# Holding prefetches behind urgent reads in a fused Fourier-mixing and ReGLU kernel

## The chip, the cores and the metric

The kernel runs on one core of a Trainium2 chip. The metric is the device time of one execution in microseconds (us), lower is better. Engines are named as in the profile: PE is TensorE (PEld its weight loads), DVE VectorE, ACT ScalarE, POOL GpSimd, SP SyncE; SPq and POOLq are the instruction streams of SP and POOL that issue DMAs.

## The reference, cut to what matters

```python
# x: 8 batches x 3008 positions x 256 channels, float32
X = np.fft.rfft(x, axis=1)
Y = X * (filt_r + 1j * filt_i)            # one filter per frequency and channel
x = np.fft.irfft(Y, n=3008, axis=1).reshape(8 * 3008, 256)
gate = np.maximum(x @ w_gate, 0.0)        # 256 -> 1536
out = (gate * (x @ w_val)) @ w_out        # 1536 -> 256
```

The kernel does the transform as two short ones, 3008 = 94 x 32. Per batch there are three stages, with a trip through device memory between them since the axes change places:

- Stage A: a product over the 94 (psA), written to `Abuf`.
- Stage B: `Abuf` is read back as the tile `at`; a product over the 32 (psX), the multiplication with the filters `Ftr` and `Fti` (tt, uu), and the product back (psD), written to `Dbuf`.
- Stage C: `Dbuf` is read back as `dC`; the product back over the 94 (psY) gives yT, the input of the gated layer.

The gated layer (psV, psG, psO) is the bulk of TensorE's work. It runs in a main loop of 47 blocks of 12 steps; the stages of the next batch are strewn between these steps. Only batch 0's stages, and part of batch 1's stage A, stand ahead of the loop, in a prologue.

## The kernel before

These are the parts that the change and the argument touch; cuts are marked with `# ...`.

```python
def load_x(b, engs, cut=None):             # x of one batch: XF[0], XF[1], 1.57 MB each, 3 DMAs each
    # ...
def load_filters():
    for src, dst in FILT:                  # (filt_r, Ftr), (filt_i, Fti)
        for a in range(2):
            # ... two DMAs: the main parts
        nc.gpsimd.dma_start(dst[64:95:2, NG - 2:, :], ...)     # two small ones
        # ...
        nc.gpsimd.dma_start(nyq[-1], ...)

def hold_gpsimd(tile_):                    # GpSimd issues nothing more until tile_ is there
    scr = pro.tile(list(tile_.shape), tile_.dtype, tag="scr", bufs=3)
    nc.gpsimd.tensor_copy(scr, tile_)

def load_at(b, c):                         # one quarter of stage B's input
    if c == 0:
        ats[b] = sb.tile([128, NG, D], BF16, tag="at", bufs=1, name="at")
    nc.sync.dma_start(ats[b][32 * c:32 * c + 32], _ap(Abuf[b], ...))

# ---- prologue
load_x(0, (nc.scalar, nc.sync), 2 * q)
# ...
hold_gpsimd(XF[0][:, 2 * q - 8:2 * q])     # first quarter of x
load_filters()
warm(14)                                   # filler products, 512 columns each
for i, f in enumerate(items_a(0)):         # stage A of batch 0
    f()
    warm(1, 256)
    # ... load_tables(), load_at(0, 0..2)
load_at(0, 3)
warm(22)
# ... place_tables, place_filter
hold_gpsimd(ats[0][96:128, NG - 1, 0:8])
load_vg(0, DFF // 3)
nc.sync.dma_start(gate, ats[0][96:128, NG - 1, 0:8])
load_x(1, (nc.sync,))
early = items_a(1)
def amid(i):                               # in stage B of batch 0
    if i < 8:
        warm(1)
    else:
        next(early)()
for f in items_b(0, amid):
    f()
load_d(0, 0, 2)
# ... a small DMA of Dbuf on gpsimd, so that what follows is held
load_vg(DFF // 3, DFF)
load_o()
for i in range(8):
    next(early)()
    warm(1, 256)
for h in range(2):
    item_c(0, h)
load_d(0, 2)

# ---- what is strewn into the main loop
C_AT = (8, 10)
for b in range(1, B):
    end = (b * S // W - 1) * NFT + C_AT[0] - 5
    s0, sb0 = (0, 13) if b == 1 else (end - 54, end - 30 | 1)
    # ... stage A from step s0
    for c in range(4):
        at_step(s0 + n - 10 + 4 * c if b > 1 else 4, lambda b=b, c=c: load_at(b, c))
    if b + 1 < B:
        at_step(sb0 + 3, lambda b=b: load_x(b + 1, (nc.gpsimd,)))
    for i, f in enumerate(items_b(b)):     # stage B from step sb0
        at_step(sb0 + 2 * i, f)
    at_step(sb0 + 27, lambda b=b: load_d(b))
```

In program order the load of the next x stands after the start of stage B. GpSimd, which issues it, does not run in that order: it has nothing else to do and issues each half of x as soon as stage A has read the buffer that it goes into.

Of the kernel before, what the change touches and what calls it, by code (L numbers as in the profile page):

```python
# [12 lines left out]
FP32 = mybir.dt.float32  # L13
# [18 lines left out]
NG = 24  # L32
# [3 lines left out]
def _ap(t, offset_elems, ap_list):  # L36
    return dataclasses.replace(
        t, offset=t.offset + offset_elems, ap=[list(p) for p in ap_list]
    )
# [63 lines left out]
def kernel(  # L103
# [10 lines left out]
    nc = tc.nc  # L114
# [16 lines left out]
    sb = ctx.enter_context(tc.tile_pool(name="sb", bufs=2))  # L131
    ps = ctx.enter_context(tc.tile_pool(name="ps", bufs=2, space=bass.MemoryType.PSUM))
    prologue = ExitStack()
    pro = prologue.enter_context(tc.tile_pool(name="pro", bufs=1))
# [6 lines left out]
    XF = [consts.tile([128, NX2 * D], FP32, name=f"XF{c}") for c in range(N2 // NX2)]  # L141
# [11 lines left out]
    def load_x(b, engs, cut=None):  # L153
        w = NX2 * D
        n = 0
        for c, xf in enumerate(XF):
            for (c0, c1) in ((0, w),) if cut is None or c else ((0, cut), (cut, w)):
                for m in range(3):
                    rows = min(32, B * N1 - (b * N1 + 32 * m))
                    n += 1  # L160
                    engs[n % len(engs)].dma_start(xf[m:m + 4 * rows - 3:4, c0:c1],  # L161
                                                  _ap(x, (b * N1 + 32 * m) * N2 * D + c * w + c0,
                                                      [[N2 * D, rows], [1, c1 - c0]]))

    H = NG // 2
    FILT = ((filt_r, Ftr), (filt_i, Fti))
# [8 lines left out]
    def place_tables(half):  # L175
        gs = slice(half * H, half * H + H)
        for a in range(2):
            nc.vector.tensor_scalar(F2[:, gs, a * 64:a * 64 + 64], tabs[:, half, 0],
                                    WA[:, NROW + a:NROW + a + 1], None, op0=ALU.mult)
            for i, t in ((1, I2t), (2, I2u)):  # L180
                nc.vector.tensor_scalar(
                    t[:, gs, :].rearrange("p g (n a c) -> p g n a c", a=2, c=2)[:, :, :, a, :],
                    tabs[:, half, i].rearrange("p g (n c) -> p g n c", c=2),
                    WA[:, NROW + 2 + a:NROW + 3 + a], None, op0=ALU.mult)
# [3 lines left out]
    def load_filters():  # L188

        for src, dst in FILT:  # L190
            for a in range(2):
                r, k1, n = a * 64, 1 + 24 * a, NG - 2 * a
                nc.gpsimd.dma_start(dst[r:r + 31:2, 0:n, :],
                                    _ap(src, k1 * D, [[N1 * D, 16], [1, n * D]]))
                nc.gpsimd.dma_start(dst[r + 1:r + 32:2, 0:n, :],
                                    _ap(src, (N1 - k1) * D, [[N1 * D, 16], [-D, n], [1, D]]))
            nc.gpsimd.dma_start(dst[64:95:2, NG - 2:, :],
                                _ap(src, 0, [[N1 * D, 16], [47 * D, 2], [1, D]]))
            nyq.append(pro.tile([1, D], BF16, tag="nyq", bufs=2, name="nyq"))
            nc.gpsimd.dma_start(nyq[-1], _ap(src, (S // 2) * D, [[D, 1], [1, D]]))  # L200
# [20 lines left out]

    def hold_gpsimd(tile_):

        scr = pro.tile(list(tile_.shape), tile_.dtype, tag="scr", bufs=3)
        nc.gpsimd.tensor_copy(scr, tile_)


    turn = {"tags": ("fft", "psv", "psg", "pso"), "i": 0}
# [1 line left out]
    def fft_tag():  # L230
        turn["i"] += 1
        return turn["tags"][turn["i"] % len(turn["tags"])]

    def items_a(b):

        def one(c, j, st):
            if j == 0:
                st["asb"] = sb.tile([NROW, NC2 * D], BF16, tag="asb", bufs=4, name="asb")
            psA = ps.tile([128, 512], FP32, tag=fft_tag(), name="psA")
            o = (c * NC2 % NX2) * D + j * 512  # L240
            nc.tensor.matmul(psA[0:NROW], WA[:, :NROW], XF[c * NC2 // NX2][:, o:o + 512],  # L241
                             start=True, stop=True)
            dst = st["asb"][:, j * 512:(j + 1) * 512]
            nc.scalar.copy(dst, psA[0:NROW])  # L244
            if j == 3:
                nc.sync.dma_start(_ap(Abuf[b], c * NROW * NC2 * D, [[NC2 * D, NROW], [1, NC2 * D]]),
                                  st["asb"])
        for c in range(N2 // NC2):
            st = {}
            for j in range(NC2 * D // 512):  # L250
                yield lambda c=c, j=j, st=st: one(c, j, st)
# [3 lines left out]
    ats = {}  # L255

    def load_at(b, c):
        if c == 0:
            ats[b] = sb.tile([128, NG, D], BF16, tag="at", bufs=1, name="at")
        nc.sync.dma_start(ats[b][32 * c:32 * c + 32],  # L260
                          _ap(Abuf[b], c * NROW * NC2 * D, [[D, 32], [4 * NC2 * D, NG], [1, D]]))

    def items_b(b, amid=None):
# [36 lines left out]
        for g in range(0, NG, 2):  # L300
            def both(g=g):
                fwd(g)
                if amid:
                    amid(g // 2)
                if len(held) > 2:
                    inv()
            yield both
# [5 lines left out]
    def load_d(b, z0=0, z1=NZ):  # L313
        for z in range(z0, z1):
            dC = sb.tile([NROW, 4, D], BF16, tag="dC", bufs=12)
            nc.sync.dma_start(dC, _ap(Dbuf[b], z * 4 * NROW * D,
                                      [[D, NROW], [NROW * D, 4], [1, D]]))
            dCs[b, z] = dC
# [68 lines left out]
    def warm(n, cols=512):  # L387

        psJ = ps.tile([128, 512], FP32, tag=fft_tag(), name="psJ")
        for i in range(n):  # L390
            nc.tensor.matmul(psJ[:, :cols], junk[:, 0:128], junk[:, :cols], start=True, stop=True)  # L391

    nc.sync.dma_start(WA, nc.inline_tensor(wa_h, name="dft_wa").ap())
    q = NX2 * D // 4
# [7 lines left out]
    load_x(0, (nc.scalar, nc.sync), 2 * q)  # L402
    for (src, dst) in FILT:
        nc.vector.memset(dst[64:128, NG - 2:, :], 0.0)
    hold_gpsimd(XF[0][:, 2 * q - 8:2 * q])
    load_filters()

    warm(14)
# [5 lines left out]
        if i % 4 == 3 and i > 3:  # L414
            load_at(0, i // 4 - 1)
    load_at(0, 3)
    warm(22)
    place_tables(0)
    place_tables(1)
    for fi in range(2):  # L420
# [2 lines left out]
    for fi in range(2):  # L423
        place_filter(fi, 0, 1, nc.scalar.copy)
        place_filter(fi, 1, 1, nc.vector.tensor_copy)
# [3 lines that stand above are left out]
# [3 lines left out]

    def amid(i):
        if i < 8:
            warm(1)
        else:
            next(early)()

    for f in items_b(0, amid):
        f()  # L440
# [17 lines left out]
    def at_step(s, f):  # L458
        side.setdefault(s, []).append(f)
# [5 lines that stand above are left out]
        a_items = early if b == 1 else items_a(b)  # L465
        n = 0
        for i, f in enumerate(a_items):
            at_step(s0 + i, f)
            n += 1
        for c in range(4):  # L470
            at_step(s0 + n - 10 + 4 * c if b > 1 else 4, lambda b=b, c=c: load_at(b, c))
        if b + 1 < B:
            at_step(sb0 + 3, lambda b=b: load_x(b + 1, (nc.gpsimd,)))
        for i, f in enumerate(items_b(b)):
            at_step(sb0 + 2 * i, f)
        at_step(sb0 + 27, lambda b=b: load_d(b))
# [42 lines left out]
```

## Time and profile before

The median is 1015.6 us (1014.9 to 1016.7). The profiled execution has a span of 1014.0 us.

| where TensorE waits for `at` | wait, us |
|---|---|
| batch 0 (prologue) | 7.67 |
| batch 1 | 15.65 |
| batches 3, 4, 5, 6 | 4.84, 2.85, 2.38, 4.78 |
| batches 2, 7 | under 1, 0 |

Two parts of the page of the kernel before matter here: busy time by engine, and the chain of work that ended last.

```profile
span 1014.0 us, 16145 instructions
PE 951.2 (94%) x5906; PEld 566.4 (56%) x6016; DVE 546.2 (54%) x823; ACT 527.0 (52%) x940; POOL 42.0 (4%) x70
...
PE 85%; DMA 11%; issue 1%; DVE 1%; ACT 1%; SPq 0%; POOL 0%; ACTq 0%
```

TensorE is the bottleneck nearly everywhere; the chain leaves it for 11% of the span, to follow DMAs. The table of waits of TensorE in the kernel before says which (total us, number of waits, longest).

```profile
PE psX L273 <- DMA at<-Abuf: 38.2, 6, 15.6
PE psA L241 <- DMA XF<-in_x_dram: 2.7, 1, 2.7
PE psJ L391 <- DVE junk L397: 2.5, 1, 2.5
PE psO L372 <- ACT osb L378: 2.5, 2, 2.0
```

Nearly all of it is stage B waiting for its input. (In batch 2 the profile names no releaser for the wait, and it is not in this table.) Here is batch 3 in the timeline of TensorE, kernel before. The columns are start, duration (merged over the instructions of the line), engine, line, operation, result and operands, count, and in brackets the idle time ahead of it and what ended it.

```profile
347.21 0.60 PE L354 MATMUL psV<-yT,WvT 128*128 128x512 bf16 x2
347.64 0.59 PE L354 MATMUL psG<-yT,WgT 128*128 128x512 bf16 x2
348.07 0.60 PE L372 MATMUL psO<-WoT,prod 128*128 128x256 bf16 x4
353.52 0.59 PE L273 MATMUL psX<-at,F 128*128 128x256 bf16 x2 [4.84 <-DMA at<-Abuf]
353.89 1.06 PE L354 MATMUL psV<-yT,WvT 128*128 128x512 bf16 x2
```

Besides the wait there is a second cost. The pair of products that took 0.60 us from first start to last end takes 1.06 us after the wait: the clock has been halved. From start to start it is 0.86 us against 0.43.

What delayed `at`? First the queue of SP around batch 3, then the issues of GpSimd, then SP's queue in batch 7, which has no next x; all of the kernel before.

```profile
337.39 1.52 SPq L246 DMA_DIRECT2D Abuf<-asb  x1
349.54 0.32 SPq L260 DMA_DIRECT2D at<-Abuf  x1
```

```profile
319.25 1.58 POOL L161 DMA_DIRECT2D XF<-in_x_dram  x3 [99.74 <-PE psA L241]
337.04 1.57 POOL L161 DMA_DIRECT2D XF<-in_x_dram  x3 [16.21 <-PE psA L241]
```

```profile
831.85 0.32 SPq L246 DMA_DIRECT2D Abuf<-asb  x1
837.60 0.32 SPq L260 DMA_DIRECT2D at<-Abuf  x1
```

SP issues the last quarter of `at` when the last quarter of `Abuf` has been written. With x issued 0.35 us ahead of it, that write (0.39 MB) takes 12.1 us; in batch 7, without x, 5.7 us. The x that is in the way will be used some 100 us later.

### The profile page before, as it was taken

Reading aid. Unit: us, or ns where it says so; the run is one execution under the profiler, and the core shown is the slowest. Engines: PE = TensorE matmul, PEld = TensorE weight load, DVE = VectorE, ACT = ScalarE, POOL = GpSimd, SP = SyncE. Lnnn points to the kernel's source line nnn. Section 1 sums busy time; section 2 is a strip of 40 time slices with the busy share of each in tenths; the row PEclk is TensorE's granted clock in tenths of the full one; section 3 lists DMA queues with packets and bytes.
Section 4 is the critical chain, followed back from the end, with each engine's and each line's share of the span. In section 5 each row is a group of like instructions: output and inputs, shape, how many; then the busy total and the mean of one; then the engine's idle time right before and its main releaser. Section 6 shows DMA issues by size and latency. Waiting matters only on the chain.

```text
span 1014.0 us, 16145 instructions
## 1 busy us (share of the span) xinstructions
PE 951.2 (94%) x5906; PEld 566.4 (56%) x6016; DVE 546.2 (54%) x823; ACT 527.0 (52%) x940; POOL 42.0 (4%) x70
## 2 busy tenths in 40 slices
PE   7693999999999899998999989999799999999995
PEld 3341666556665466645665456655466556666664
DVE  3632765347653376534865358543575437755552
ACT  3561555555555455554555545555365555555552
POOL 3330000000000000000000000001000000000000
PEclk9796999999999999999999999999899999999999
DMA  9899132261234412454222551416324232241111
GB/s 263 224 227 236 53 100 57 64 223 52 75 98 149 141 39 78 96 158 133 63 78 71 160 141 54 124 51 170 101 58 122 60 99 64 55 110 41 32 32 43
DMA packets 94432, 106.29 MB, mean 105 GB/s; under 512 B 7796, under 2 KB 84724, under 8 KB 92660
## 3 DMA queue, kind: packets, MB, share of 16 engines
q1 hardware_dynamic: 87520, 80.03, 29.8%
q0 software_dynamic: 6240, 22.71, 8.1%
q10 hardware_dynamic: 592, 2.51, 0.7%
q8 instruction: 47, 0.77, 0.3%
q14 instruction: 33, 0.27, 0.1%
HBM read 59.32 MB, written 49.81 MB: 108 GB/s over the span
## 4 chain that ended last, share of the span: by engine, by line
PE 85%; DMA 11%; issue 1%; DVE 1%; ACT 1%; SPq 0%; POOL 0%; ACTq 0%
PE psG L354 22%; PE psO L372 22%; PE psV L354 21%; PE psA L241 10%; DMA Abuf<-asb 7%; DMA at<-Abuf 3%; PE psX L273 2%; PE psD L293 2%; PE psD L292 2%; PE psY L338 2%; DMA XF<-in_x_dram 1%; DMA out_dram<-osb 1%; ACT vsb L357 0%; DVE prod L359 0%; PE psJ L391 0%
## 5 line engine op out<-in xcount | busy, mean ns | idle before, releaser
L359 DVE SCALAR_TENSOR_TENSOR prod<-psG,vsb 128x512 bf16<-128x512 f32 x564 | 390.1, 692 | 374.9 <-ACT vsb L357 357.6
L357 ACT CAST vsb<-psV 128x512 bf16<-128x512 f32 x564 | 331.3, 587 | 252.5 <-PE psV L354 209.8
L372 PE MATMUL psO<-WoT,prod 128*128 128x256 bf16 x2256 | 338.8, 274 | 4.0 <-ACT osb L378 2.5
L354 PE MATMUL psG<-yT,WgT 128*128 128x512 bf16 x1098 | 331.4, 381 | 4.4 <-DMA WgT<-in_moe_w_gate_dram 0.6
L354 PE MATMUL psV<-yT,WvT 128*128 128x512 bf16 x1049 | 321.7, 382 | 1.7 <-ACT yT L343 0.6
L372 PEld LDWEIGHTS <-prod 128*128 128x128 bf16 x2256 | 221.7, 98 | 148.7 <-issue 6.4
L354 PEld LDWEIGHTS <-WgT 128*128 128x128 bf16 x1128 | 110.6, 98 | 136.9 <-issue 4.4
L354 PEld LDWEIGHTS <-WvT 128*128 128x128 bf16 x1128 | 104.8, 98 | 60.2 <-issue 49.7
L241 PE MATMUL psA<-XF,WA 128*96 128x512 f32 x256 | 129.6, 592 | 2.7 <-DMA XF<-in_x_dram 2.7
L244 ACT CAST asb<-psA 96x512 bf16<-96x512 f32 x128 | 74.4, 582 | 104.8 <-PE psA L241 101.4
L276 DVE TENSOR_TENSOR tt<-psX,Ftr 128x512 bf16<-128x512 f32 x96 | 65.5, 683 | 38.4 <-PE psX L273 38.3
L295 ACT CAST dsb<-psD 128x512 bf16<-128x512 f32 x96 | 56.1, 587 | 52.9 <-PE psD L293 51.4
L273 PE MATMUL psX<-at,F 128*128 128x256 bf16 x192 | 38.5, 284 | 39.1 <-DMA at<-Abuf 38.2
L378 ACT COPY osb<-psO 128x512 f32<-128x512 f32 (+1 forms) x96 | 55.4, 577 | 33.7 <-PE psO L372 26.1
L282 DVE TENSOR_TENSOR uu<-psX,Fti 128x512 bf16<-128x512 f32 x90 | 61.3, 681 | 0.0
L293 PE MATMUL psD<-uu,I2u 128*128 128x256 bf16 x192 | 47.7, 275 | 0.5 <-POOL uu L280 0.5
L292 PE MATMUL psD<-tt,I2t 128*128 128x256 bf16 x192 | 47.8, 276 | 0.0
L161 POOL DMA_DIRECT2D XF<-in_x_dram x36 | 19.0, 532 | 625.6 <-PE psA L241 625.4
L273 PEld LDWEIGHTS <-F 128*128 128x128 bf16 x192 | 18.9, 100 | 43.9 <-issue 25.6
L338 PEld LDWEIGHTS <-dC 96*128 96x128 bf16 x604 | 35.3, 99 | 13.5 <-issue 10.8
L241 PEld LDWEIGHTS psA<-XF,WA 128*96 128x96 f32 x256 | 35.1, 163 | 12.2 <-issue 5.9
L345 DVE CAST yT<-psY 128x512 bf16<-128x512 f32 x47 | 32.2, 685 | 17.8 <-PE psY L338 17.8
(45 smaller groups left out, 181.8 us busy)
## 6 DMA issues: line engine op xcount, KB each, us to landing
XF<-in_x_dram POOLq DMA_DIRECT2D x34, 512.0 KB, 8.4
Abuf<-asb SPq DMA_DIRECT2D x32, 384.0 KB
at<-Abuf SPq DMA_DIRECT2D x32, 384.0 KB
dC<-Dbuf SPq DMA_DIRECT2D x64, 192.0 KB
Dbuf<-dsb SPq DMA_DIRECT2D x31, 384.0 KB
out_dram<-osb SPq DMA_DIRECT2D x72, 94.0 KB
XF<-in_x_dram SPq DMA_DIRECT2D x8, 512.0 KB
tabs<-dft_tab ACTq DMA_DIRECT2D x2, 576.0 KB
```

The lines of the kernel that those rows point to most:

```text
L241: nc.tensor.matmul(psA[0:NROW], WA[:, :NROW], XF[c * NC2 // NX2][:, o:o + 512], start=True, stop=True)
L244: nc.scalar.copy(dst, psA[0:NROW])
L273: nc.tensor.matmul(psX[:, i], F2[:, g + i, :], at[:, g + i, :], start=True, stop=True)
L276: nc.vector.tensor_tensor(tt, psX, Ftr[:, g:g + 2, :], op=ALU.mult)
L282: nc.vector.tensor_tensor(uu, psX, Fti[:, g:g + 2, :], op=ALU.mult)
L292: nc.tensor.matmul(psD[:, i], I2t[:, g + i, :], tt[:, i], start=True, stop=False)
L293: nc.tensor.matmul(psD[:, i], I2u[:, g + i, :], uu[:, i], start=False, stop=True)
L295: nc.scalar.copy(st["dsb"][:, o:o + 2, :], psD)
L354: nc.tensor.matmul(pt[:, :W], w[:, h, ft * 128:(ft + 1) * 128], yt[:, h, :], start=(h == 0), stop=(h == 1))
L357: nc.scalar.copy(vsb, psV[:, :W])
L359: nc.vector.scalar_tensor_tensor(prod, in0=psG[:, :W], scalar=0.0, in1=vsb, op0=ALU.max, op1=ALU.mult)
L372: nc.tensor.matmul(psO[:, t % 2], prods[ft][:, t * 128:(t + 1) * 128], WoT[:, ft, :], start=(ft == 0), stop=(ft == NFT - 1))
```

## The change

The intent is to let urgent transfers go first. The next x is held, by a small copy on GpSimd, until the last quarter of `at` has landed. In the prologue the filters are held until the first half of x (before: its first quarter) has landed, and their large parts are issued ahead of the small ones. Then there are two tunings of fillers, products on a constant tile that are meant to keep TensorE's clock up: 26 instead of 22 ahead of stage B of batch 0, and 128 instead of 512 columns within it. The whole diff:

```diff
--- before.py
+++ after.py
@@ -194,6 +194,7 @@
                                     _ap(src, k1 * D, [[N1 * D, 16], [1, n * D]]))
                 nc.gpsimd.dma_start(dst[r + 1:r + 32:2, 0:n, :],
                                     _ap(src, (N1 - k1) * D, [[N1 * D, 16], [-D, n], [1, D]]))
+        for src, dst in FILT:
             nc.gpsimd.dma_start(dst[64:95:2, NG - 2:, :],
                                 _ap(src, 0, [[N1 * D, 16], [47 * D, 2], [1, D]]))
             nyq.append(pro.tile([1, D], BF16, tag="nyq", bufs=2, name="nyq"))
@@ -221,8 +222,8 @@
 
     def hold_gpsimd(tile_):
 
-        scr = pro.tile(list(tile_.shape), tile_.dtype, tag="scr", bufs=3)
-        nc.gpsimd.tensor_copy(scr, tile_)
+        scr = sb.tile([128, 8], FP32, tag="scr", bufs=2)
+        nc.gpsimd.tensor_copy(scr[:tile_.shape[0]], tile_)
 
 
     turn = {"tags": ("fft", "psv", "psg", "pso"), "i": 0}
@@ -402,7 +403,7 @@
     load_x(0, (nc.scalar, nc.sync), 2 * q)
     for (src, dst) in FILT:
         nc.vector.memset(dst[64:128, NG - 2:, :], 0.0)
-    hold_gpsimd(XF[0][:, 2 * q - 8:2 * q])
+    hold_gpsimd(XF[0][:, 4 * q - 8:])
     load_filters()
 
     warm(14)
@@ -414,7 +415,7 @@
         if i % 4 == 3 and i > 3:
             load_at(0, i // 4 - 1)
     load_at(0, 3)
-    warm(22)
+    warm(26)
     place_tables(0)
     place_tables(1)
     for fi in range(2):
@@ -432,7 +433,7 @@
 
     def amid(i):
         if i < 8:
-            warm(1)
+            warm(1, 128)
         else:
             next(early)()
 
@@ -470,7 +471,10 @@
         for c in range(4):
             at_step(s0 + n - 10 + 4 * c if b > 1 else 4, lambda b=b, c=c: load_at(b, c))
         if b + 1 < B:
-            at_step(sb0 + 3, lambda b=b: load_x(b + 1, (nc.gpsimd,)))
+            def next_x(b=b):
+                hold_gpsimd(ats[b][96:128, NG - 1, 0:8])
+                load_x(b + 1, (nc.gpsimd,))
+            at_step(sb0 + 1, next_x)
         for i, f in enumerate(items_b(b)):
             at_step(sb0 + 2 * i, f)
         at_step(sb0 + 27, lambda b=b: load_d(b))
```

## The prediction

> **What bounds the kernel now.** TensorE: busy 951 of 1014 us (page, part 1), 85% of the chain that ended last. In the table of waits it waits 38.2 us, six times, in front of stage B's first product (psX) for the DMA that lands its input (at<-Abuf). By batch, from the timeline: 7.67 us (batch 0), 15.6 (1), none to speak of in 2, 4.84, 2.85, 2.38, 4.78 (3 to 6), none in 7. Batch 7 is the only one with no further x to load. Its last Abuf write took 5.7 us from its issue until the read behind it could be issued; in batches 3 to 6 the same write took 12.1, 10.3, 9.8 and 12.1 us, with the second half of the next x issued within 0.5 us of it. So x's 3 MB is in the way of 0.8 MB that is urgent.
>
> The waits also cost clock. After the 4.84 us wait two 128x512 matmuls take 0.85 us instead of 0.43 for about 4.5 us. The Trainium skill ("TensorE: Matmul & The Clock Gate", The HAM clock gate) says an idle window of about 3.4 us halves the clock until it has been busy that long; the trace agrees: 2.38 us left no mark, 2.85 us some (about 1.7 us lost).
>
> **Later batches.** The change holds x behind the landing of the last quarter of at; x is used some 100 us later. Written in 5.7 us and read in 3.9, at arrives about 1.4 us ahead of TensorE in batches 3 to 6. Waits saved: 14.9 us; cold clock: about 2.2+1.7+2.2, say 6. Together 21 us, all on TensorE's chain. The holds are 0.2 us copies on idle GpSimd. x will now run beside Dbuf and output writes; at most 1 us of that comes back.
>
> **Batch 1.** From 60 to 98 us the DMA engines are saturated (busy share about 1.0 in the windows) and move 9.3 MB, of which x is 3.1. At the 277 GB/s that GpSimd's queue reaches for its own share, x is worth 11 us. So at lands at about 87 instead of 98.3, while TensorE arrives at 82.7: some 4 us of wait stay, since weights and dC are still in front. Saved: 11 us of wait and 1 of cold clock: 12.
>
> **Start, batch 0.** Holding the filters until XF[0] is complete (about 2.5 us later) gives x the engines: the 2.7 us wait of psA for the second half of x should mostly go. But DMA is saturated from 7 to about 33 us, and filters and tables are needed before stage B too, so the wait for at mostly moves: stage B starts 2 us earlier. Fillers of 128 instead of 512 columns save 0.32 us (cold) or 0.16 (warm) each, at most 1.9 us over eight; batch 1's x, needed at 48.8, may take part of that back. warm(26) adds 0.9 us inside a wait: nothing. Together 3 us (0 to 6).
>
> **Sum.** 21 + 12 + 3 = 36, less 1 for contention: about 980 us. Range 969 to 992. Faster by over 2%: 0.94; within 2%: 0.05; slower: 0.01.
>
> **What would show it.** Waits of psX for at: about 0 in batches 3 to 6, 0 to 6 us in batch 1, 4 to 8 in batch 0. Last Abuf write of batches 3 to 6 about 6 us. GpSimd's x issues right after at has landed. psA's wait for x under 1 us.
>
> **What would make it wrong.** Output writes or Dbuf writes, not x, slow the Abuf writes; the late x stalls the output buffers; late filters hold stage B of batch 0; batch 1's weights alone keep at beyond 90 us.

## The result and the profile after

The changed kernel takes 984.8 us in the median (984.2 to 986.1, 4 runs) against 1015.6 us. The ratio is 0.9697, with a 95% interval of 0.9681 to 0.9714. (Ratios are the mean time of one kernel's fast runs over that of the other's of the same rounds, so not quite the ratio of the medians.)

The same parts of the page, and the table of waits of TensorE, for the changed kernel:

```profile
span 982.2 us, 16279 instructions
PE 951.0 (97%) x6020; PEld 565.2 (58%) x6020; DVE 544.9 (55%) x823; ACT 526.7 (54%) x940; POOL 42.9 (4%) x76
...
PE 91%; DMA 5%; SPq 1%; ACT 0%; issue 0%; DVE 0%; POOL 0%; ACTq 0%; POOLq 0%
```

```profile
PE psX L274 <- DMA at<-Abuf: 16.3, 3, 8.2
...
PE psO L373 <- ACT osb L379: 2.5, 2, 2.0
PE psD L294 <- POOL uu L281: 1.5, 2, 1.0
PE psG L355 <- DMA WgT<-in_moe_w_gate_dram: 1.3, 1, 1.3
```

TensorE's busy time looks the same to 0.2 us, but these two figures can't be compared: 110 products are missing from the records of the kernel before (5906 products for 6016 weight loads), none from these. In the second profile of the changed kernel (see below), where 110 are missing too, TensorE is busy for 944.8 us, 6.4 us less than before. So some of the gain is in the products themselves, which ran at the low clock for less time; the rest is waits. The waits for `at` fell from 38.2 to 16.3 us. psA's wait for x (2.7 us) is gone in this profile, and small new waits stand in its place, for GpSimd's product uu and for weights. The wait for output buffers (psO for osb) is as it was, so the later x did not stall them.

GpSimd's issues around batch 3, and SP's last write and read of batches 3 and 5, changed kernel:

```profile
339.09 0.18 POOL L226 CAST scr<-at 32x8 f32<-32x8 bf16 x1 [118.04 <-DMA at<-Abuf]
339.60 3.16 POOL L161 DMA_DIRECT2D XF<-in_x_dram  x6 [0.33 <-PE psX L274]
```

```profile
326.92 1.43 SPq L247 DMA_DIRECT2D Abuf<-asb  x1
334.69 0.32 SPq L261 DMA_DIRECT2D at<-Abuf  x1
...
564.12 0.32 SPq L247 DMA_DIRECT2D Abuf<-asb  x1
569.85 0.32 SPq L261 DMA_DIRECT2D at<-Abuf  x1
```

x now leaves 0.5 us after `at` has landed. The last write takes 7.8, 6.1, 5.7 and 5.6 us in batches 3 to 6, as against 12.1, 10.3, 9.8 and 12.1. Batch 3 keeps a wait of 0.79 us, batches 4 to 6 none.

Where the 31.8 us of the two profiles came from is read best from the start of stage B of each batch, in the timelines of TensorE of both kernels:

| first psX of batch | before, us | changed, us | lead, us |
|---|---|---|---|
| 0 | 38.76 | 37.36 | 1.4 |
| 1 | 98.34 | 89.55 | 8.8 |
| 2 | 230.39 | 219.92 | 10.5 |
| 3 | 353.52 | 339.00 | 14.5 |
| 4 | 477.17 | 457.13 | 20.0 |
| 5 | 599.51 | 575.27 | 24.2 |
| 6 | 722.58 | 693.40 | 29.2 |
| 7 | 843.00 | 811.53 | 31.5 |
| end | 1014.0 | 982.2 | 31.8 |

Batches 3 to 7 give 21.0 us (31.5 less 10.5), batch 1 with the low clock after it and the wait of 0.95 us in batch 2, which went too, 9.1 (10.5 less 1.4), and the start 1.4 us. What is left in the changed kernel is the wait of 8.15 us in the prologue and that in batch 1; here is TensorE's timeline of the latter:

```profile
81.63 0.60 PE L373 MATMUL psO<-WoT,prod 128*128 128x256 bf16 x4
89.55 0.61 PE L274 MATMUL psX<-at,F 128*128 128x256 bf16 x2 [7.33 <-DMA at<-Abuf]
89.95 1.06 PE L355 MATMUL psV<-yT,WvT 128*128 128x512 bf16 x2
```

And the queue of SP in front of it, changed kernel:

```profile
59.06 4.08 SPq L247 DMA_DIRECT2D Abuf<-asb  x2
63.18 8.39 SPq L317 DMA_DIRECT2D dC<-Dbuf  x6
71.67 1.60 SPq L247 DMA_DIRECT2D Abuf<-asb  x1
73.38 8.78 SPq L261 DMA_DIRECT2D at<-Abuf  x4
```

### The profile page after: what moved, and what is told of

Its sections match the earlier page's. It is cut to its first block, busy times and chain, and to the rows that moved or that the text cites. A ratio compares the mean times of both kernels' runs of the same rounds, so it can differ in the third digit from the quotient of the medians.

```text
span 982.2 us, 16279 instructions
## 1 busy us (share of the span) xinstructions
PE 951.0 (97%) x6020; PEld 565.2 (58%) x6020; DVE 544.9 (55%) x823; ACT 526.7 (54%) x940; POOL 42.9 (4%) x76
## 4 chain that ended last, share of the span: by engine, by line
PE 91%; DMA 5%; SPq 1%; ACT 0%; issue 0%; DVE 0%; POOL 0%; ACTq 0%; POOLq 0%
PE psO L373 24%; PE psV L355 24%; PE psG L355 24%; PE psA L242 10%; DMA Abuf<-asb 3%; PE psX L274 2%; PE psY L339 2%; PE psD L294 2%; PE psD L293 2%; DMA at<-Abuf 2%; SPq L317 1%; PE psJ L392 1%; DMA out_dram<-osb 0%; ACT asb L245 0%; POOL uu L281 0%
## 5 line engine op out<-in xcount | busy, mean ns | idle before, releaser
L355 PE MATMUL psG<-yT,WgT 128*128 128x512 bf16 x1128 | 335.8, 379 | 1.3 <-DMA WgT<-in_moe_w_gate_dram 1.3
L355 PE MATMUL psV<-yT,WvT 128*128 128x512 bf16 x1128 | 336.2, 379 | 0.8 <-ACT yT L344 0.6
L274 PE MATMUL psX<-at,F 128*128 128x256 bf16 x192 | 38.1, 283 | 16.3 <-DMA at<-Abuf 16.3
L344 ACT CAST yT<-psY 128x512 bf16<-128x512 f32 x47 | 27.5, 586 | 19.6 <-PE psY L339 19.5
L339 PE MATMUL psY<-M,dC 96*128 96x94 bf16 (+18 forms) x604 | 37.5, 198 | 0.0
```

The lines of the kernel that those rows point to most:

```text
L274: nc.tensor.matmul(psX[:, i], F2[:, g + i, :], at[:, g + i, :], start=True, stop=True)
L339: nc.tensor.matmul(psY[:, o:o + w], dCs[b, n2 // 4][:, n2 % 4, h * 128:(h + 1) * 128], M1[:, n1:n1 + w], start=True, stop=True)
L355: nc.tensor.matmul(pt[:, :W], w[:, h, ft * 128:(ft + 1) * 128], yt[:, h, :], start=(h == 0), stop=(h == 1))
```

## The experiments

Twelve kernels ran. Each is shown as its diff against the changed kernel, unless another is named (lines with - are the changed kernel's). Each ran beside the kernel before on the same chip; the median of that kernel was 1013.7 to 1015.4 us from call to call, so small differences are only drawn between kernels of one call.

Theory 1: the hold on x is nearly the whole gain, and the other parts give almost nothing, since the lead of 1.4 us at batch 0 has shrunk to 0.5 us when TensorE comes to wait in batch 1 (at 82.69 us before, 82.22 changed). The rival is the prediction's sum: 3 us from the start.

### The hold on x alone

This is the kernel before with only the hold on x added. Seen from the changed kernel, that undoes all the rest:

```diff
@@ -196,3 +196,2 @@
                                     _ap(src, (N1 - k1) * D, [[N1 * D, 16], [-D, n], [1, D]]))
-        for src, dst in FILT:
             nc.gpsimd.dma_start(dst[64:95:2, NG - 2:, :],
@@ -405,3 +404,3 @@
         nc.vector.memset(dst[64:128, NG - 2:, :], 0.0)
-    hold_gpsimd(XF[0][:, 4 * q - 8:])
+    hold_gpsimd(XF[0][:, 2 * q - 8:2 * q])
     load_filters()
@@ -417,3 +416,3 @@
     load_at(0, 3)
-    warm(26)
+    warm(22)
     place_tables(0)
@@ -435,3 +434,3 @@
         if i < 8:
-            warm(1, 128)
+            warm(1)
         else:
```

> The kernel before with one part of the change: the next x held until at has landed; filters and fillers as before. Theory 1 (the hold on x is nearly the whole gain, the parts at the start almost nothing, since their 1.4 us at batch 0 shrink to 0.5 us before batch 1): 985 to 986 us. Theory 2 (each part gives what the prediction said, 3 us for the start): 988 us. In both the waits of batches 3 to 6 for at are under 1 us and psA's wait of 2.7 us for x in batch 0 is back.

Measured: 983.8 us (981.2 to 984.8), ratio 0.9684 (0.9664 to 0.9705); waits in batches 3 to 6 of 0.3 us in all, psA waits 1.7 us for x in batch 0. All of the gain is there.

### All but the hold on x

```diff
@@ -473,6 +473,3 @@
         if b + 1 < B:
-            def next_x(b=b):
-                hold_gpsimd(ats[b][96:128, NG - 1, 0:8])
-                load_x(b + 1, (nc.gpsimd,))
-            at_step(sb0 + 1, next_x)
+            at_step(sb0 + 3, lambda b=b: load_x(b + 1, (nc.gpsimd,)))
         for i, f in enumerate(items_b(b)):
```

> The changed kernel with x not held: filters held and reordered, fillers small. Theory 1: 1014 to 1015.5 us, 0 to 1.5 us gained. Theory 2: 1012 to 1013 us. Waits for at in batches 1 and 3 to 6 as in the kernel before (15, 4.8, 2.9, 2.4, 4.8 us).

Measured: 1014.0 us, ratio 0.9994 (0.9976 to 1.0012); in the profile, of its fastest execution (1011.4 us), waits of 16.1 us in batch 1 and 4.8, 3.0, 2.3 and 3.3 us in batches 3 to 6. Theory 1 holds: the parts at the start are worth 0.6 us by the middle of the interval and 2.4 us by its end.

### The fillers of before

```diff
@@ -417,3 +417,3 @@
     load_at(0, 3)
-    warm(26)
+    warm(22)
     place_tables(0)
@@ -435,3 +435,3 @@
         if i < 8:
-            warm(1, 128)
+            warm(1)
         else:
```

> The changed kernel with the fillers of before (22 products of 512 columns, and 512 columns instead of 128 in stage B of batch 0). Theory 1: the small fillers leave TensorE idle between groups (0.96 and 0.52 us waits for GpSimd), the clock stays low 7.7 us instead of 5.8 us, and nothing is gained: 984.3 to 985.3 us, the low clock ends about 6 us after stage B starts. Theory 2 (as predicted, fillers worth 1 to 2 us): 986 to 987 us.

Measured: 983.6 us, ratio 0.9694 (0.9674 to 0.9714), beside 983.8 us of the hold alone and a ratio of 0.9697 of the changed kernel. No gain from the small fillers is to be seen. Stage B of batch 0 comes to the first psA of batch 1 9.5, 9.7 and 10.05 us after its start in the three profiles with the large fillers (this run, the hold alone, the kernel before), and after 9.5 to 10.3 us in the nine profiles with the small fillers and at most 26 products of filler ahead. So the smaller products did not shorten the stage. That the stage is longer with them, as theory 1 had it, is not shown either: the two spreads overlap.

### Only the second half of x held

```diff
@@ -152,3 +152,3 @@
 
-    def load_x(b, engs, cut=None):
+    def load_x(b, engs, cut=None, only=None):
         w = NX2 * D
@@ -156,2 +156,4 @@
         for c, xf in enumerate(XF):
+            if only is not None and c != only:
+                continue
             for (c0, c1) in ((0, w),) if cut is None or c else ((0, cut), (cut, w)):
@@ -474,4 +476,5 @@
             def next_x(b=b):
+                load_x(b + 1, (nc.gpsimd,), only=0)
                 hold_gpsimd(ats[b][96:128, NG - 1, 0:8])
-                load_x(b + 1, (nc.gpsimd,))
+                load_x(b + 1, (nc.gpsimd,), only=1)
             at_step(sb0 + 1, next_x)
```

> The changed kernel with only the second half of the next x held until at has landed; the first half goes as soon as its buffer is free, some 18 us before the last Abuf write. Theory 1 (only what is in flight beside the last Abuf write and the last at read costs): batches 3 to 6 wait under 1 us for at, their last Abuf write takes about 6 us; batch 1, where the engines are saturated from 60 us on, waits 5 us longer than in the changed kernel (12 to 13 us); in all 989 to 991 us. Rival (any x ahead of at costs, since it delays the earlier quarters too): waits of 1 to 3 us in batches 3 to 6 as well, 994 to 1000 us.

Measured: 989.2 us (987.5 to 990.4), ratio 0.9747 (0.9727 to 0.9767). The waits of TensorE in this run, with 12.06 us of them in batch 1, 8.55 in batch 0 and 0.99 in batch 3:

```profile
PE psX L276 <- DMA at<-Abuf: 21.6, 3, 12.1
```

In batches 3 and 4 the first half of x left 18 us ahead of the last write of `Abuf`, and that write took 7.8 and 6.1 us, as with all of x held. So in the steady state only the half issued beside the last write had to be held. Batch 1 is different: there the first half costs. This run is a dose. `at` of batch 1 lets stage B begin at 98.3 us with both halves in front (kernel before), 93.8 with one, 89.6 with none: 4.6 and 4.2 us for 1.57 MB each. The kernel before has another start, though; the run of all but the hold, which has the same start, begins at 96.6 us. Counted from the issue of the last `Abuf` write, which itself moves by 2 us between these profiles, it is 25.8 us (before) and 25.9 (all but the hold) with both halves in front, 22.4 with one and 17.9 with none: 3.5 and 4.5 us.

### What is left in batch 1

The changed kernel still waits 7.3 us there. Theory S: the DMA engines are saturated (the profile's share is 1.07 from 63 to 71.6 us and 1.24 from 71.6 to 81.6) and the bytes in front decide. Rival L: the reads are issued too late, and run into the last write. Three runs bear on it.

```diff
@@ -449,5 +449,9 @@
         warm(1, 256)
+        if i == 5:
+            load_at(1, 0)
     for h in range(2):
         item_c(0, h)
-    load_d(0, 2)
+    load_d(0, 2, 4)
+    load_at(1, 1)
+    load_d(0, 4)
     prologue.close()
@@ -471,3 +475,4 @@
         for c in range(4):
-            at_step(s0 + n - 10 + 4 * c if b > 1 else 4, lambda b=b, c=c: load_at(b, c))
+            if b > 1 or c > 1:
+                at_step(s0 + n - 10 + 4 * c if b > 1 else 2 * c - 2, lambda b=b, c=c: load_at(b, c))
         if b + 1 < B:
```

> The changed kernel with the four reads of batch 1's stage B input (at) issued as soon as each quarter of Abuf is written, among the dC loads, instead of all four behind the last write. Bytes in front unchanged. Theory S (the engines are saturated from 63 us on and the bytes in front decide): batch 1 still waits 5 to 7 us, time within 2 us of the changed kernel's 984. Rival L (it is the late issue: three reads and the last write run into one another): the last write takes 6 to 7 us and the last read 4 us, the wait falls to 0 to 3 us, time 977 to 980 us.

Measured: 986.95 us, ratio 0.9724 (0.9703 to 0.9746): worse than either said, with a wait of 9.6 us. The queue of SP in this run shows why:

```profile
64.60 3.26 SPq L261 DMA_DIRECT2D at<-Abuf  x1
67.91 8.70 SPq L317 DMA_DIRECT2D dC<-Dbuf  x4
76.64 2.43 SPq L261 DMA_DIRECT2D at<-Abuf  x1
79.17 1.99 SPq L247 DMA_DIRECT2D Abuf<-asb  x1
87.12 0.30 SPq L261 DMA_DIRECT2D at<-Abuf  x1
```

SP issues in order. The reads now stand ahead of the last write, which left at 79.2 us instead of 71.7, though ScalarE had its data ready at 70.1 us. The experiment is a miss: it does not tell S from L. It does show that the place in the queue costs too: with the same bytes the wait grew by 2.3 us. This fits what the Trainium skill says ("DMA: Bandwidth & Descriptors", Anatomy of one DMA): DMA engines do not wait on semaphores, the issuing sequencer does, ahead of dispatch. So what SP has yet to issue waits with it.

```diff
@@ -451,3 +451,3 @@
         item_c(0, h)
-    load_d(0, 2)
+    load_d(0, 2, 4)
     prologue.close()
@@ -480,2 +480,3 @@
         at_step(sb0 + 27, lambda b=b: load_d(b))
+    at_step(5, lambda: load_d(0, 4))
     prev = None
```

> The changed kernel with four of the six dC loads that stand in front of the last Abuf write on the same queue moved behind the last at read (0.79 MB in 512-byte pieces). Theory S: the wait of batch 1 falls by 3 to 5 us to 2 to 4 us, and the low clock after it shrinks: 978 to 981 us. Rival L: the wait falls by under 1.5 us, 983 to 984 us.

Measured: 982.4 us, ratio 0.9685 (0.9664 to 0.9706). Stage B of batch 1 began at 86.95 us, 2.6 us earlier than in the changed kernel, with a wait of 5.25 us. That is in the direction of S, but short of its 3 to 5 us; and the change in the time against the changed kernel is not clear of noise (its own runs gave 0.9697 and 0.972).

```diff
@@ -428,2 +428,3 @@
     load_vg(0, DFF // 3)
+    load_o()
     nc.sync.dma_start(gate, ats[0][96:128, NG - 1, 0:8])
@@ -445,3 +446,2 @@
     load_vg(DFF // 3, DFF)
-    load_o()
     for i in range(8):
```

> The changed kernel with the output weights loaded right behind the first third of the other weights, at 39 us, instead of at 60 us: 0.79 MB (1.57 MB read) leave the stretch in front of batch 1's stage B. Theory S: the wait of batch 1 falls by 2 to 4 us, and the wait for WgT (1.3 us) falls too, but batch 1's x lands later and psA, at 47.7 us, waits 1 to 3 us: 981 to 984 us. If weights on the other queue hardly slow the chain Abuf, at: the wait of batch 1 stays above 6.5 us.

Measured: 981.9 us, ratio 0.968 (0.966 to 0.9699). The wait of batch 1 fell to 2.5 us, but stage B began at 88.9 us, hardly sooner: TensorE was held up on its way there, 1.9 us by dC in stage C of batch 0 and 1.5 us by WgT, and behind the first of these the granted clock was 0.50 from 65.2 to 68.6 us. psA did not wait for x, as had been expected; the earlier weights delayed the writes of `Dbuf` instead (the first dC was issued at 61.7 us instead of 58.2). Here, in a saturated stretch, moving a transfer mostly moved the wait.

Together: bytes in front of batch 1 cost time (the dose of x, and dC in part), and so does order. How the 7.3 us divide between the two stays open.

### What bounds the start

```diff
@@ -146,3 +146,3 @@
     Ftr = consts.tile([128, NG, D], BF16)
-    Fti = consts.tile([128, NG, D], BF16)
+    Fti = Ftr
     WgT = consts.tile([128, 2, DFF], BF16)
@@ -165,3 +165,3 @@
     H = NG // 2
-    FILT = ((filt_r, Ftr), (filt_i, Fti))
+    FILT = ((filt_r, Ftr),)
     tabs = pro.tile([128, 2, 3, H, 64], BF16, tag="tabs", bufs=1)
@@ -420,6 +420,6 @@
     place_tables(1)
-    for fi in range(2):
+    for fi in range(1):
         for a in range(2):
             place_filter(fi, a, 0, nc.vector.tensor_copy)
-    for fi in range(2):
+    for fi in range(1):
         place_filter(fi, 0, 1, nc.scalar.copy)
```

> Wrong result on purpose: the second filter is not loaded, its place is taken by the first (0.77 MB less written, 1.54 MB less read in the first 30 us). If bytes bound the start (as the prediction said), at of batch 0 lands 3 to 5 us earlier than at 37.2 us and the time falls by 2 to 5 us. Rival: the chain itself (last x, TensorE's stage A until 23.5 us, one write, one read) bounds it, and the filters' bytes are by then out of the way: at lands within 1.5 us of before.

Measured, with a wrong result as intended: 981.4 us, ratio 0.967 (0.9646 to 0.9694). Stage B of batch 0 began at 33.8 us instead of 37.4, and batch 1's at 86.7 instead of 89.6. So the prediction's reading of the start is supported by the time at which `at` landed: bytes bound it, and a change of their order, which beside the fillers is all that the change makes there, has little to win. The time as a whole is not clear of noise against the changed kernel (0.9697, 0.9681 to 0.9714).

### Giving TensorE other work in batch 1

If `at` cannot come sooner, stage B can begin later; the main loop has other products to do. The changed kernel was run again as a base.

> The changed kernel once more, as the base of the two runs beside it: 984 us, ratio 0.970.

Measured: 985.3 us (984.3 to 986.3), ratio 0.972 (0.970 to 0.9741), with a 7.39 us wait in batch 1.

```diff
@@ -464,3 +464,3 @@
         end = (b * S // W - 1) * NFT + C_AT[0] - 5
-        s0, sb0 = (0, 13) if b == 1 else (end - 54, end - 30 | 1)
+        s0, sb0 = (0, 19) if b == 1 else (end - 54, end - 30 | 1)
         a_items = early if b == 1 else items_a(b)
```

> The changed kernel with batch 1's stage B begun six steps of the main loop later, so that TensorE has some 8 us of other products to do while at is on its way. If the 7.3 us wait of batch 1 and the low clock after it are what is left there, both go: no wait over 1 us in batch 1, 974 to 977 us. If at is pushed back by the change of order, or dC of batch 1 then comes too late for stage C, the wait stays or a new one appears: above 980 us.

Measured: 976.3 us (974.5 to 976.8), ratio 0.9627 (0.9606 to 0.9648), 9.0 us below the run beside it. TensorE's timeline in front of batch 1's stage B in this run, and the top of its waits:

```profile
89.81 0.59 PE L355 MATMUL psG<-yT,WgT 128*128 128x512 bf16 x2
90.24 0.60 PE L373 MATMUL psO<-WoT,prod 128*128 128x256 bf16 x4
90.67 0.38 PE L274 MATMUL psX<-at,F 128*128 128x256 bf16 x2
```

```profile
PE psX L274 <- DMA at<-Abuf: 10.3, 2, 9.3
PE psO L373 <- ACT osb L379: 2.8, 2, 2.3
```

Stage B begins at 90.7 us, 0.7 us later than in the base (90.0), without a wait and at the full clock; the two waits left are batch 0's (9.3) and 1.0 us in batch 3. The wait of 7.4 us makes up most of the 9.0 us. The rest is about what the low clock behind it cost, which is gone too: in the base the granted clock was 0.50 for the first 3.4 us of the stage, a loss of some 1.7 us.

### The clock in stage B of batch 0

The two last runs put more fillers into batch 0's wait, on top of the previous edit. The first, against the previous run:

```diff
@@ -417,3 +417,3 @@
     load_at(0, 3)
-    warm(26)
+    warm(58)
     place_tables(0)
```

> The same with 58 instead of 26 products of filler in front of batch 0's stage B, which end about 36 us, just before at lands. If the low clock costs there, it is granted in full from the start of stage B, which then reaches batch 1's first psA 1 to 2.5 us sooner (8 to 9 us after its start instead of 10.3), and the time falls by as much against the run beside it. If VectorE and GpSimd pace this stage, the full clock gains under 0.7 us.

Measured: 975.1 us (974.9 to 975.9), ratio 0.9622 (0.9602 to 0.9642): not to be told from the run beside it. The first psA came 10.1 us after the start of stage B. The stage did not get the full clock that it was to have, as the table of stretches of this run shows (start and end; length; busy us and count of PE, PEld, DVE, ACT and POOL in this order; granted clock; DMA share; GB/s):

```profile
37.00:40.00 3.00, 0.98 (x9) 0.82 (x10) 0.63 (x2) 0.00 (x0) 0.87 (x2) 1.00 0.15 23
40.00:43.00 3.00, 1.81 (x8) 1.07 (x8) 2.88 (x6) 1.66 (x3) 1.77 (x3) 0.58 0.84 126
43.00:46.00 3.00, 2.78 (x15) 1.99 (x15) 1.09 (x3) 1.33 (x3) 1.36 (x3) 0.50 1.11 317
46.00:49.00 3.00, 2.66 (x20) 2.00 (x19) 2.25 (x4) 1.99 (x4) 2.24 (x2) 0.79 1.04 383
```

The stage begins at full clock and loses it at 40.4 us, 1.5 us after the wait of 3.38 us that TensorE still had in front of it. Between 40 and 43 us TensorE is busy 1.81 of 3 us, with VectorE busy 2.88; its longest wait there is 0.96 us, for GpSimd's uu. Either the wait ahead or these gaps may have cost the clock. The last run gives the fillers their 512 columns back:

```diff
@@ -435,3 +435,3 @@
         if i < 8:
-            warm(1, 128)
+            warm(1)
         else:
```

> The run with batch 1's stage B later and 58 fillers, now with fillers of 512 columns in stage B of batch 0 again. In the run with fillers of 128 columns the clock was full at the start of stage B and fell to 0.5 between 40 and 46 us, with idle TensorE between the groups. If the small fillers are why it fell, the clock stays at 0.9 or more from 37 to 49 us, batch 1's first psA comes 8 to 9 us after the start of stage B instead of 10.1, and the time is 973 to 975 us, ratio 0.961. If VectorE and GpSimd alone pace the stage, the clock stays up but psA still comes 10 us after the start: 975 to 976 us.

Measured: 974.6 us (974.5 to 976.9), ratio 0.9608 (0.9589 to 0.9626). The same stretches:

```profile
37.00:40.00 3.00, 1.05 (x6) 0.66 (x7) 0.63 (x2) 0.00 (x0) 0.88 (x2) 0.93 0.21 32
40.00:43.00 3.00, 3.00 (x12) 1.66 (x11) 2.42 (x5) 1.66 (x3) 1.77 (x3) 0.50 0.80 164
43.00:46.00 3.00, 2.73 (x22) 1.98 (x21) 2.09 (x5) 1.81 (x4) 1.88 (x3) 1.00 1.09 299
```

The expectation was wrong in part: the clock fell here too, behind the 2.93 us that TensorE still waited, but it was low for 3.4 us (39.6 to 43.0) and not for 6.8 (40.4 to 47.3), and psA came 9.4 us after the start. One profile of each shows no more than that. In the other profiles the low clock ended 3.0 to 9.6 us after the start of stage B with small fillers (nine profiles) and 3.9 to 5.9 us after it with large ones (three), so that small fillers hold the clock down is not shown. What all profiles show is a longest wait for uu of 0.95 us or more with small fillers and of at most 0.46 us with large ones. The time cannot be told from that of the two runs before it, whose intervals it overlaps. What is shown is that all three versions with stage B of batch 1 begun later beat both kernels; the ordering among the three is not.

## Why the prediction was right

The predicted 980 us, range 969 to 992, hold the measured 984.8. Its steps:

- **x is in the way of the last write (21 us, batches 3 to 6).** Right, in mechanism and size: 21.0 us in the table of leads. The hold alone gives all the gain, and the run without it gives none that is clear of noise. The four waits went from 14.9 to 0.8 us; the other 7 us are the low clock behind them, which the prediction had sized at 6. Apart from the waits the lead grew by 2.7, 1.8 and 2.3 us behind those of batches 3, 4 and 6, where the granted clock of the kernel before was 0.50 for 5.2, 3.4 and 4.7 us, and by 0.2 us behind that of batch 5, where it stayed full. That the sum came out to the tenth is luck: the waits gave 0.8 us less than predicted and the clock 0.9 more. What the prediction quoted of the Trainium skill ("TensorE: Matmul & The Clock Gate", The HAM clock gate) agrees with the trace in the halving: 0.86 us for a pair of products after a wait of 4.84 us, against 0.43. It does not agree in the length of the window, since 2.85 us were enough (see the end). That a transfer issued by GpSimd can slow one issued by SP fits what the skill states ("DMA: Bandwidth & Descriptors", Issuing engines are not separate DMA queues): both run on the same 16 engines and interleave. Here that is 12.1 us against 5.7 for one write.
- **Batch 1 (12 us).** Mechanism right, size off: 9.1 us. The mis-sized term is "x is worth 11 us". The runs showed 8.0 us for the whole of x, in two doses of 3.5 and 4.5, counted from the last `Abuf` write (8.8 us by the clock time at which stage B starts). The estimate divided x's bytes by the average rate of GpSimd's queue (277 GB/s: 22.7 MB in 8.1% of the span); taking the 3.1 MB away gained at about 350 to 390 GB/s (3.1 MB by 8.8 or 8.0 us). So `at` let stage B begin at 89.6 us instead of about 87, and a wait of 7.3 us stayed instead of 4. The low clock behind it stayed as well, for 3.2 us of stage B against 4.3 before, where the prediction had counted 1 us as saved.
- **The start (3 us, 0 to 6).** The profile gives 1.4 us at stage B of batch 0 (the second profile of the changed kernel 0.6), and the paired runs give nothing clear of noise. That the wait "mostly moves" was right: psA's 2.7 us for x went (1.3 us of it came back in the second profile of the same kernel, and 1.9 in the run with the late dC, whose start is the same), and the wait for `at` grew from 7.67 to 8.15 us. The term for the fillers (at most 1.9 us) came out as nothing: the stage took 10.05 us to the first psA before and 10.3 us in the changed kernel. It counted the columns that were taken away, and left out that TensorE then waits for GpSimd (1.5 us in the changed kernel, 0.5 before) and that smaller fillers also keep TensorE less busy; whether that cost clock, the last two runs leave open.
- **Contention of the late x (1 us).** Not seen: the waits of psO for osb are 2.5 us in both kernels.

## What to carry to other kernels

An idle engine that issues prefetches does so at the first moment that a buffer is free, and that moment is often when the last, urgent transfer of the same stage leaves: hold the prefetch on the landing of the urgent one, by a tiny copy on the issuing engine. Compare the duration of the urgent transfer in a round with and one without the prefetch to know beforehand what the hold is worth. Where the stretch is saturated and the wait cannot be moved, start the consumer later and let the engine do other work, which here gained 9 us more.

## What the Trainium skill lacked or had wrong

- "TensorE: Matmul & The Clock Gate": it gives one idle window of about 3.4 us as the idle time that halves the clock. Here waits of 2.85 us (batch 4, before) and 2.93 us (last run) were enough, while 2.38 us (batch 5, before) was not. The low clock set in only about 1 us after work had resumed (at 478.1 us after a wait that ended at 477.2).
- The same page has no figure for how busy TensorE must be, in a stretch of several short waits, to keep its clock. Here it lost it (0.50 from 65.2 us, run with the early output weights) behind waits of 1.61 and 0.27 us, having been busy for 1.53 of the 3.41 us before; the single wait of 2.38 us of batch 5 did not cost it.
- "DMA: Bandwidth & Descriptors", Issuing engines are not separate DMA queues: it calls the time that a sequencer takes to issue a DMA usually small relative to the DMA itself. In the saturated stretch SP needed 8.4 us to issue six dC loads, and 0.85 us for the two a few us earlier; what waits behind them in the queue pays for it. The trace does not show what holds the issue up.
- No page has a figure for what one ordinary stream of DMAs costs an urgent one of the same core. Here 1.57 MB of large rows in front of `at` cost 3.5 to 4.6 us in the saturated stretch, and the same 1.57 MB beside one write of 0.39 MB 3.1 to 6.5 us (7.8 to 12.1 us in batches 2 to 6 before, against 4.7 to 7.8 in the same batches of the changed kernel).
